# SwiGLU feed-forward on one core: the last 256 output columns move from VectorE and the SP queue to ScalarE and the ACT queue

## The chip, the cores and the metric

The kernel runs on one core of a Trainium2 chip. The metric is the device time of one execution in microseconds (us). One executed kernel gives one time. A profiled execution gives a trace as well, with the start and the duration of every instruction.

A few words are used throughout. The **span** is the time from the first to the last instruction in the trace, 121.1 us for the kernel before. The **tail** is the time from the end of the last matmul to the end of the span. A **semaphore** is a counter that one instruction raises and another waits for. A transfer has **landed** when its semaphore has its last count; the **closing** is the time from the landing of the last store to the end of the span. A **slab** is a block of weight columns that one transfer loads. The times outside the timeline views, given to the nanosecond below, are from the instruction records of the same traces (their starts, ends, semaphore waits and DMA landings).

## The reference

```python
# x: (1, 2048, 512), w_gate and w_up: (512, 1376), w_down: (1376, 512), all bfloat16
def reference(x, w_gate, w_up, w_down):
    g = jax.nn.silu(x @ w_gate)
    u = x @ w_up
    return (g * u) @ w_down
```

## The kernel before

The token axis is cut into four chunks of 512. For each chunk and each 128 columns of F, TensorE computes gate and up into two PSUM banks, ScalarE takes the Silu, VectorE multiplies, and the product stays in SBUF. Then come 16 output tiles of 128 tokens; each takes 11 matmuls, a copy out of PSUM, and a store. The last tile is cut into two groups of 256 columns, so that the last copy and store are short.

```python
N_WARM = 11
# ... (buffers and semaphores cut)
        o_groups = []                        # (tile, first column, columns)
        for t in range(NST):                 # NST = 16
            if t == NST - 1:
                o_groups.append((t, 0, HD))  # HD = 256
                o_groups.append((t, HD, HD))
            else:
                o_groups.append((t, 0, D))   # D = 512
        NOG = len(o_groups)                  # 17

        @block.sync
        def _(sp):
            xT_dma(sp, 0)                    # x, transposed on the way
            for si in range(len(slabs)):     # five slabs of gate and up columns
                wg_slab_dma(sp, si)
                wu_slab_dma(sp, si)
            # ... (the other loads cut)
            n_store = [0] * NOS              # NOS = 3 output buffers
            for gi, (t, c0, ncol) in enumerate(o_groups):
                ob = og_buf(gi)
                if gi == NOG - 2:
                    sp.wait_ge(s_Ofa, 1)     # ScalarE copied the next-to-last group
                elif gi == NOG - 1:
                    sp.wait_ge(s_Of, gi)
                else:
                    sp.wait_ge(s_Of, gi + 1)
                sp.dma_start(of[t * P:(t + 1) * P, c0:c0 + ncol],
                             o_sb[ob][:, c0:c0 + ncol]).then_inc(s_out[ob], 16)
                n_store[ob] += 1
            for i in range(NOS):             # the end waits for every buffer's stores
                sp.wait_ge(s_out[i], 16 * n_store[i])

        @block.tensor
        def _(pe):
            for i in range(N_WARM):          # warm-up matmuls on constants
                pe.matmul(banks[7][:, :], lhsT=ones_w, rhs=ones_m, start=True, stop=True)
            # ... for each chunk c and column tile ft:
            #     wait x chunk, wait gate slab, 4 matmuls; wait up slab, 4 matmuls
            # ... then 11 matmuls for each of the o_groups

        @block.scalar
        def _(act):
            # ... (the Silus cut)
            gi = NOG - 2                     # ScalarE copies the next-to-last group
            # ...
            act.activation(o_sb[ob][:, c0:c0 + ncol], psO[bb][:, 0:ncol], ACT.Copy).then_inc(s_Ofa, 1)

        @block.vector
        def _(dve):
            # ... (the products cut)
            for gi, (t, c0, ncol) in enumerate(o_groups):
                if gi == NOG - 2:
                    continue
                # ... waits
                dve.tensor_copy(o_sb[ob][:, c0:c0 + ncol], psO[bb][:, 0:ncol]).then_inc(s_Of, 1)
```

## Time and profile before

| what | value |
|---|---|
| time | 122.78 us, median of 3 runs (122.36 to 122.86) |
| span of the profiled run | 121.1 us |
| TensorE busy | 117.9 us, 97% |
| before the first real matmul | 5.5 us |
| from there to the end of the last matmul | 113.1 us |
| tail | 2.49 us |

First the page of the kernel before: the span, the busy time of each engine with its share and number of instructions, and the chain of waits that ended last.

```profile
span 121.1 us, 1391 instructions
## 1 busy us (share of the span) xinstructions
PE 117.9 (97%) x550; PEld 53.3 (44%) x550; DVE 43.8 (36%) x64; ACT 30.2 (25%) x51; POOL 0.2 (0%) x4
...
PE 97%; DVE 0%; issue 0%
```

TensorE is the limit, and nothing else comes near it. Next, the same kernel cut into three stretches, head, middle and tail (start:end, length, then busy time and instructions of each engine, the granted clock, the share and rate of the DMA):

```profile
0.00:5.50 5.50, 4.73 (x11) 1.47 (x11) 0.00 (x0) 1.49 (x2) 0.20 (x4) 1.00 0.71 154
5.50:118.66 113.16, 113.16 (x540) 51.79 (x539) 43.40 (x63) 28.74 (x49) 0.00 (x0) 1.00 0.24 67
118.66:121.15 2.49, 0.00 (x0) 0.00 (x0) 0.42 (x1) 0.00 (x0) 0.00 (x0) 1.00 0.18 53
```

In the middle TensorE is busy for the whole of the 113.16 us: no copy, Silu or store is waited for there. In the head it is busy too, but with eleven warm-up matmuls on constants. In the tail only one short copy is counted as busy; the rest is a store on its way. The tail in the timeline (start, length, engine; SPq is SyncE's DMA queue, and the length of a DMA line is the time to issue it, not to move the data), and the time to landing of that last store:

```profile
118.69 0.42 DVE L308 CAST o_sb<-bank 128x256 bf16<-128x256 f32 x1 [1.72 <-PE bank L245]
119.15 0.33 SPq L156 DMA_DIRECT2D out_dram<-o_sb  x1
```

```profile
out_dram<-o_sb SPq DMA_DIRECT2D x1, 64.0 KB, 1.5
```

The matmul ends at 118.655, the copy takes 0.425, the store is issued at 119.146 and lands at 120.667, and 0.480 us more pass until the last instruction of the closing barrier has ended. So a chain that the page counts as "0%" takes 2.49 us, and the chain of waits on the page stops at the copy.

### The profile page before, as it was taken

How to read it: one execution, taken by the hardware profiler on the slowest of the kernel's cores; microseconds unless marked ns; L12 is line 12 of the kernel's file. 1: busy time of each engine (PE TensorE's matmuls, PEld its weight loads, DVE VectorE, ACT ScalarE, POOL GpSimd, SP SyncE). 2: the span in 40 equal slices, each digit the busy share in tenths (PEclk: the TensorE clock that was granted, in tenths of full speed). 3: DMA queues.
4: the chain of work that ended last, by engine and by line, in shares of the span. 5: the costliest groups of instructions: out<-in, count | busy, mean ns of one | idle time of the engine just before them, and what ended most of it. 6: DMA issues, size and time to landing. Idle time of an engine off the chain costs nothing.

```text
span 121.1 us, 1391 instructions
## 1 busy us (share of the span) xinstructions
PE 117.9 (97%) x550; PEld 53.3 (44%) x550; DVE 43.8 (36%) x64; ACT 30.2 (25%) x51; POOL 0.2 (0%) x4
## 2 busy tenths in 40 slices
PE   7999999999999999999999999999999999999991
PEld 2244444444444444444444444444444444444470
DVE  0024334444334444334444334467242233224221
ACT  4032333262333272333262333230000000000010
POOL 0000000000000000000000000000000000000000
PEclk9999999999999999999999999999999999999999
DMA  3999999900000000000000000000211211121121
GB/s 67 255 283 372 262 241 225 369 20 0 0 0 0 0 0 5 0 0 3 3 0 0 0 0 0 5 0 0 87 43 43 87 43 49 49 81 43 43 74 56
DMA packets 17990, 8.51 MB, mean 70 GB/s; under 512 B 11360, under 2 KB 17984, under 8 KB 17984
## 3 DMA queue, kind: packets, MB, share of 16 engines
q1 hardware_dynamic: 17984, 8.42, 25.6%
q8 instruction: 4, 0.07, 0.2%
q14 instruction: 2, 0.02, 0.0%
HBM read 4.23 MB, written 2.10 MB: 52 GB/s over the span
## 4 chain that ended last, share of the span: by engine, by line
PE 97%; DVE 0%; issue 0%
PE bank L245 32%; PE bank L179 29%; PE bank L191 29%; PE bank L167 4%; PE bank L204 3%; PE bank L215 2%; DVE o_sb L308 0%; PE bank L220 0%
## 5 line engine op out<-in xcount | busy, mean ns | idle before, releaser
L284 DVE TENSOR_TENSOR hT_sb<-sg_sb,bank 128x512 bf16<-128x512 f32 x40 | 27.5, 688 | 44.9 <-PE bank L191 44.8
L179 PE MATMUL bank<-xT_sb,w_sb 128*128 128x512 bf16 x160 | 41.5, 382 | 0.0
L191 PE MATMUL bank<-xT_sb,w_sb 128*128 128x512 bf16 x160 | 41.1, 379 | 0.0
L245 PE MATMUL bank<-wd_sb,hT_sb 128*128 128x512 bf16 (+3 forms) x187 | 38.3, 367 | 0.0
L261 ACT ACTIVATE sg_sb<-bank 128x512 f32<-128x512 f32 x40 | 23.8, 596 | 44.7 <-PE bank L179 44.7
L245 PEld LDWEIGHTS bank<-wd_sb,hT_sb 128*128 128x128 bf16 (+1 forms) x187 | 18.1, 97 | 20.3 <-issue 0.4
L179 PEld LDWEIGHTS bank<-xT_sb,w_sb 128*128 128x128 bf16 x160 | 15.6, 98 | 19.8 <-DMA xT_sb<-in_x_dram 0.8
L191 PEld LDWEIGHTS bank<-xT_sb,w_sb 128*128 128x128 bf16 x160 | 15.6, 98 | 18.9
L308 DVE CAST o_sb<-bank 128x512 bf16<-128x512 f32 (+1 forms) x16 | 10.8, 675 | 24.9 <-PE bank L245 24.9
L275 ACT ACTIVATE o_sb<-bank 128x256 bf16<-128x256 f32 x1 | 0.4, 383 | 37.6 <-PE bank L245 37.6
L167 PE MATMUL bank<-const-bfloat16-1.0 128*128 128x512 bf16 x11 | 4.9, 628 | 0.8 <-PEq L322 0.8
L289 DVE TENSOR_TENSOR hT_sb<-sgx_sb,bank 32x512 bf16<-32x512 f32 x4 | 2.8, 692 | 5.3 <-ACT sgy_sb L266 5.3
L204 PE MATMUL bank<-xT_sb,w_sb 128*128 128x512 bf16 x16 | 4.1, 379 | 0.0
L265 ACT ACTIVATE sgx_sb<-bank 32x512 f32<-32x512 f32 x4 | 2.4, 588 | 4.5 <-PE bank L204 4.5
L167 PEld LDWEIGHTS bank<-const-bfloat16-1.0 128*128 128x128 bf16 x11 | 1.5, 140 | 3.3 <-issue 3.3
L296 DVE TENSOR_TENSOR hT_sb<-sgy_sb,bank 64x512 bf16<-64x512 f32 x4 | 2.7, 684 | 0.1
L204 PEld LDWEIGHTS bank<-xT_sb,w_sb 128*128 128x128 bf16 x16 | 1.6, 98 | 1.9
L266 ACT ACTIVATE sgy_sb<-bank 64x512 f32<-64x512 f32 x4 | 2.4, 589 | 0.0
L215 PE MATMUL bank<-xT_sb,w_sb 128*64 128x512 bf16 x8 | 1.9, 382 | 0.0
L220 PE MATMUL bank<-xT_sb,w_sb 128*64 128x512 bf16 x8 | 1.9, 382 | 0.0
L254 ACT ACT_TABLE_LOAD x1 | 1.3, 1283 | 0.7 <-PEq L322 0.7
L215 PEld LDWEIGHTS bank<-xT_sb,w_sb 128*64 128x64 bf16 x8 | 0.8, 110 | 1.0 <-issue 0.4
(6 smaller groups left out, 1.4 us busy)
## 6 DMA issues: line engine op xcount, KB each, us to landing
out_dram<-o_sb SPq DMA_DIRECT2D x15, 128.0 KB, 1.7
wd_sb<-in_w_down_dram SPq DMA_DIRECT2D x1, 1280.0 KB, 6.3
w_sb<-in_w_gate_dram SPq DMA_DIRECT2D x1, 480.0 KB, 6.2
w_sb<-in_w_up_dram SPq DMA_DIRECT2D x1, 448.0 KB, 6.8
w_sb<-in_w_gate_dram SPq DMA_DIRECT2D x1, 384.0 KB, 4.8
w_sb<-in_w_up_dram SPq DMA_DIRECT2D x1, 384.0 KB, 5.4
w_sb<-in_w_gate_dram SPq DMA_DIRECT2D x2, 128.0 KB, 3.1
w_sb<-in_w_up_dram SPq DMA_DIRECT2D x2, 128.0 KB, 3.0
```

The lines of the kernel that those rows point to most:

```text
L167: pe.matmul(banks[7][:, :], lhsT=ones_w, rhs=ones_m, start=True, stop=True)
L179: ins = pe.matmul(psG[n % NG][:, :], lhsT=w_sb[:, dk, ft * P:(ft + 1) * P], rhs=xT_sb[:, dk, c * SC:(c + 1) * SC], start=(dk == 0), stop=( ...
L191: ins = pe.matmul(psU[n % NU][:, :], lhsT=w_sb[:, dk, UPH + ft * P:UPH + (ft + 1) * P], rhs=xT_sb[:, dk, c * SC:(c + 1) * SC], start=(dk = ...
L204: ins = pe.matmul(psX[:, :], lhsT=w_sb[:, dk, XC0:XC0 + P], rhs=xT_sb[:, dk, c * SC:(c + 1) * SC], start=(dk == 0), stop=(dk == KD - 1),)
L215: pe.matmul(psY[pi][0:64, :], lhsT=w_sb[:, dk, YC0:YC0 + 64], rhs=xT_sb[:, dk, a * SC:(a + 1) * SC], start=(dk == 0), stop=(dk == KD - 1), ...
L245: ins = pe.matmul(psO[bb][:, 0:ncol], lhsT=hT_sb[0:K, fk, t * P:(t + 1) * P], rhs=wd_sb[0:K, fk, c0:c0 + ncol], start=(fk == 0), stop=(fk ...
L261: act.activation(sg_sb[n % NSG][:, :], psG[n % NG][:, :], ACT.Silu).then_inc(s_Gf, 1)
L265: act.activation(sgx_sb[c][96:128, :], psX[64:96, :], ACT.Silu)
L284: dve.tensor_tensor(hT_sb[:, ft, c * SC:(c + 1) * SC], sg_sb[n % NSG][:, :], psU[n % NU][:, :], ALU.mult,).then_inc(s_Uf, 1)
L289: dve.tensor_tensor(hT_sb[64:96, NFF, c * SC:(c + 1) * SC], sgx_sb[c][96:128, :], psX[96:128, :], ALU.mult,).then_inc(s_Xd, 1)
L296: dve.tensor_tensor(hT_sb[0:64, NFF, c * SC:(c + 1) * SC], sgy_sb[c][y0:y1, :], psY[pi][y0:y1, :], ALU.mult,).then_inc(s_Yd, 1)
L308: dve.tensor_copy(o_sb[ob][:, c0:c0 + ncol], psO[bb][:, 0:ncol]).then_inc(s_Of, 1)
```

## The change

What it can take is a little of the tail: ScalarE's copy of 256 columns takes 0.383 us in the trace and VectorE's 0.425, and the ACT queue saves handing the store to another engine. Most of the diff rewrites the kernel in a small recording layer, with one counting semaphore per engine and one per DMA. The instructions and their order on each engine stay as they were, except at the end (550 matmuls before and after). TensorE's separate semaphore instructions fall from 22 to 13. The core of the diff:

```diff
+class _Plan:                       # records operations with what they depend on
+    # ... op(), dma() cut
+    def emit(self, name, handle):
+        seen = {}
+        for o in self.lists[name]:
+            # ... collect the semaphores and counts that o.deps stand for
+            for k, (s, v) in need.items():
+                if seen.get(k, 0) < v:
+                    handle.wait_ge(s, v)
+                    seen[k] = v
+            # ... emit the instruction, then_inc its engine's or its DMA's semaphore
 ... (all operations rewritten as op(...) and dma(...) calls, in the same order)
-            gi = NOG - 2
-            act.activation(o_sb[ob][:, c0:c0 + ncol], psO[bb][:, 0:ncol], ACT.Copy).then_inc(s_Ofa, 1)
-                if gi == NOG - 2:
-                    continue
-                dve.tensor_copy(o_sb[ob][:, c0:c0 + ncol], psO[bb][:, 0:ncol]).then_inc(s_Of, 1)
-            for i in range(NOS):
-                sp.wait_ge(s_out[i], 16 * n_store[i])
+            last = gi == NOG - 1
+            cps = [copy("act" if last else "dve", c0, c0 + ncol)]
+            store("act" if last else "sp", 0, P, cps)
+            freed.append(cps)
+        for e in ("sp", "act"):
+            plan.lists[e].append(_Op(e, None, [s for t in range(NST - NOS, NST) for s in stores[t] if s.eng == e], False))
```

## The prediction

> **What bounds the kernel now.** TensorE. The page gives PE 117.9 us busy, 97% of a 121.1 us span, with the granted clock at full in every slice, and the chain of waits is 97% PE. In the trace's instruction records the matmuls start gap-free from 5.54 us to the last one, which ends at 118.655 us: 216 ns from start to start for 512 columns, 109 ns for 256, and only about 0.2 us lost in all, at the two places where the 64-column matmuls begin and end. Everything before 5.5 us (warm-up matmuls, first loads) and after 118.66 us is head and tail. The time of 122.78 us is the span plus about 1.7 us that the records do not cover.
>
> **What the change does.** The instruction order on each engine is the same before and after (550 matmuls, the same loads in the same order on the SP queue), except at the end. Most of the diff is a new recording layer: one counting semaphore per engine and one per DMA instead of named ones. TensorE has 22 separate semaphore instructions before and 13 after. As the present ones cause no gap in the matmul starts, removing nine of them is worth nothing. The three slots of the output tiles are waited for at the end before as well, so "the end waits only for the last three tiles" removes no wait that matters. What is left:
> - the next-to-last 256 columns are now copied by VectorE (before: ScalarE, 0.383 us). The last group's matmuls run 1.2 us after it, so this is hidden;
> - the last 256 columns are copied by ScalarE and stored from the ACT queue (before: VectorE, 0.425 us, stored from SP).
>
> **The tail, the only critical part that changes.** Before, from the timeline: last matmul ends 118.655; VectorE copy 118.693 to 119.118; SP issues the store at 119.146 and is busy 0.332 us; the store lands at 120.667 (1.52 us from issue); SP's branch, the drain and the barrier end at 121.147. After: ScalarE starts 0.037 us after its matmul in the present trace, takes 0.383, and its own queue should start the store about 0.03 us later: the store is issued some 0.04 us earlier. The Trainium skill (DMA: Bandwidth & Descriptors, "HWDGE ordering") says that SP and ACT own one ring each on the same 16 engines, so I expect the same 1.5 us to landing; its fixed cost (about 2 us, mostly the write receipt, same page) is not shortened by changing the queue, and the trace's 1.5 us is what I use. Against it: this is the first transfer on the ACT queue. On SP, the first plain load took 0.664 us to issue against 0.507 for later ones, and the first store 0.373 against 0.332, so a cold issue may cost 0.04 to 0.2 us. Net: -0.04 + 0.1 us, that is, nothing that three runs spreading over 0.5 us can show.
>
> **Predicted: 122.8 us, 8 in 10 between 122.3 and 123.3.** Faster by over 2%: 0.01; within 2%: 0.98; slower by over 2%: 0.01.
>
> **What would show each step.** Matmuls from about 5.5 to 118.7 us without gaps, as before; ACT copy of 128x256 at about 118.7 us, 0.38 us long; one 64 KB issue from the ACT queue at 119.1 us, 0.33 to 0.5 us long, landing about 1.5 us later; span 121.0 to 121.4 us; SP's own last store landed by 119.5 us, so the closing barrier waits on ACT.
>
> **What would make it wrong.** A slow first issue or landing on the ACT queue (over 0.5 us extra); a fixed cost outside the span for using a second queue; the new semaphores opening gaps between matmuls, for instance a wait now tied to a later count of the same engine; a later start of the first real matmul, which would shift everything.

## More of the kernel before

One more stretch will matter: the first real weight loads of TensorE in the timeline of its weight loads (in brackets, how long the engine sat idle, and what ended it), and the first gate slab's time from issue to landing.

```profile
4.57 0.15 PEld L167 LDWEIGHTS bank<-const-bfloat16-1.0 128*128 128x128 bf16 x1 [0.28 <-issue]
5.51 0.14 PEld L179 LDWEIGHTS bank<-xT_sb,w_sb 128*128 128x128 bf16 x2 [0.79 <-DMA xT_sb<-in_x_dram]
5.92 0.15 PEld L179 LDWEIGHTS bank<-xT_sb,w_sb 128*128 128x128 bf16 x1 [0.28 <-issue]
6.35 0.11 PEld L179 LDWEIGHTS bank<-xT_sb,w_sb 128*128 128x128 bf16 x1 [0.28 <-issue]
6.58 0.10 PEld L191 LDWEIGHTS bank<-xT_sb,w_sb 128*128 128x128 bf16 x1
```

```profile
w_sb<-in_w_gate_dram SPq DMA_DIRECT2D x1, 128.0 KB, 3.2
```

The loads follow one another at about 0.43 us until 6.35 and then at 0.22: the array runs at half speed at first. And the bracket blames the load of x for the wait, but that matmul waits for two loads: x landed at 4.92 us, the gate slab at 5.405 (2.20 plus 3.2). The semaphore instruction for the slab passed at 5.433, so the slab, not x, let TensorE go. A wait for several semaphores has to be checked against the landings.

## The result

| | before | after |
|---|---|---|
| time, median (lowest to highest), 4 runs each | 122.82 us (122.36 to 122.95) | 122.67 us (122.49 to 122.91) |
| ratio | | 0.9999, 95% interval 0.9975 to 1.0022 |
| span of the profiled run | 121.147 us | 121.034 us |
| end of the last matmul | 118.655 us | 118.548 us |
| tail | 2.492 us | 2.486 us |

A ratio is the mean time of one kernel's runs over the mean of the other's in the same rounds, so it is not quite the ratio of the medians. The page of the kernel after:

```profile
span 121.0 us, 1373 instructions
## 1 busy us (share of the span) xinstructions
PE 117.1 (97%) x540; PEld 53.3 (44%) x550; DVE 43.8 (36%) x64; ACT 30.2 (25%) x51; POOL 0.2 (0%) x4
...
PE 97%; issue 1%; ACT 0%
```

The 0.8 us less of PE time is no gain: ten matmul records are missing (x540 against x550), and in nine of the ten places the starts are 432 ns apart, two steps of 216 (the tenth lies beside the 64-column matmuls). The weight loads are all there. The tail and the landing of its store, then TensorE's first weight loads and the first gate slab:

```profile
118.58 0.38 ACT L254 ACTIVATE o_sb<-bank 128x256 bf16<-128x256 f32 x1 [38.85 <-PE bank L247]
119.00 0.37 ACTq L259 DMA_DIRECT2D out_dram<-o_sb  x1
```

```profile
out_dram<-o_sb ACTq DMA_DIRECT2D x1, 64.0 KB, 1.6
```

```profile
5.56 0.14 PEld L166 LDWEIGHTS bank<-xT_sb,w_sb 128*128 128x128 bf16 x2 [0.84 <-DMA xT_sb<-in_x_dram]
5.97 0.60 PEld L166 LDWEIGHTS bank<-xT_sb,w_sb 128*128 128x128 bf16 x3 [0.28 <-issue]
```

```profile
w_sb<-in_w_gate_dram SPq DMA_DIRECT2D x1, 128.0 KB, 3.3
```

Term by term, the copy is 41 ns shorter, the store takes 62 ns longer from issue to landing (of which 38 in the issue itself), and the closing is 28 ns shorter. These sum to -7 ns, and the tails differ by -6. The hand-over from the copy to the store, which the ACT queue was to save, took 28 ns before and 30 after. The last matmul, however, ended 107 ns earlier although the first real one had started 47 ns later. From the ninth real weight load to the end of the last matmul both kernels take 111.21 us. So that difference arose before the ninth load, where TensorE has the same instructions in the same order in both.

**Theory.** The tail is a chain of copy, issue, landing and closing, all of it on the critical path; the change shortens one term and lengthens another. The layer is free. What else differs is the head, which varies from run to run. **Rivals.** (1) The layer gives something back to TensorE and the new tail takes it. (2) The tail is not what ends the program. (3) The landing is only noise, not a matter of the queue.

### The profile page after: what moved, and what is told of

Same layout as the page of the kernel before. It is cut to its first block, busy times and chain, and to the rows that moved or that the text cites. A ratio compares the mean times of both kernels' runs of the same rounds, so it can differ in the third digit from the quotient of the medians.

```text
span 121.0 us, 1373 instructions
## 1 busy us (share of the span) xinstructions
PE 117.1 (97%) x540; PEld 53.3 (44%) x550; DVE 43.8 (36%) x64; ACT 30.2 (25%) x51; POOL 0.2 (0%) x4
## 4 chain that ended last, share of the span: by engine, by line
PE 97%; issue 1%; ACT 0%
PE bank L166 60%; PE bank L247 31%; PE bank L163 4%; PE bank L221 2%; ACT o_sb L254 0%
## 5 line engine op out<-in xcount | busy, mean ns | idle before, releaser
L166 PE MATMUL bank<-xT_sb,w_sb 128*128 128x512 bf16 x330 | 72.6, 380 | 0.3
L221 PE MATMUL bank<-xT_sb,w_sb 128*64 128x512 bf16 x16 | 1.9, 382 | 0.0
```

The lines of the kernel that those rows point to most:

```text
L166: return op("pe", lambda e: e.matmul(bank[:, :], lhsT=w_sb[:, dk, col0:col0 + P], rhs=xT_sb[:, dk, c * SC:(c + 1) * SC], start=(dk == 0), ...
L221: ym = op("pe", lambda e, pi=pi, dk=dk, c=c, y0=y0, y1=y1: e.matmul(psY[pi][y0:y1, :], lhsT=w_sb[:, dk, YC0:YC0 + 64], rhs=xT_sb[:, dk, c ...
```

## The experiments

Twelve kernels were run, in three batches of four; the four of a batch share a chip and the runs of the kernel before. All gave correct results. The terms of the tail are collected here, in ns, from the instruction records; the issue is part of the time from issue to landing, and what a row lacks to its tail are two hand-overs (matmul to copy, copy to issue), together 62 to 70 ns in every row.

| kernel | copy | issue | issue to landing | landing to end | tail |
|---|---|---|---|---|---|
| before | VectorE 425 | SP 332 | 1521 | 480 | 2492 |
| after | ScalarE 384 | ACT 370 | 1583 | 452 | 2486 |
| tail_only | ScalarE 384 | ACT 374 | 1575 | 448 | 2474 |
| queue_only | VectorE 426 | ACT 371 | 1586 | 448 | 2530 |
| copy_only | ScalarE 383 | SP 332 | 1533 | 555 | 2533 |
| copy_only_order | ScalarE 383 | SP 333 | 1527 | 476 | 2449 |
| old_tail_new_layer | VectorE 425 | SP 332 | 1529 | 554 | 2573 |
| wait_all | ScalarE 384 | ACT 369 | 1574 | 443 | 2469 |
| warm_queue | ScalarE 384 | ACT 339 | 1549 | 443 | 2443 |
| last_512 | ScalarE 597 | ACT 374 | 1744 | 448 | 2855 |
| last_128 | ScalarE 278 | ACT 369 | 1505 | 444 | 2294 |
| combined | ScalarE 278 | ACT 338 | 1472 | 444 | 2260 |

### tail_only: the tail without the layer

```diff
 # the kernel before
-            gi = NOG - 2
+            gi = NOG - 1
             act.activation(..., ACT.Copy).then_inc(s_Ofa, 1)
+            act.wait_ge(s_Ofa, 1)
+            act.dma_start(of[...], o_sb[ob][...]).then_inc(s_outa, 16)
+            act.wait_ge(s_outa, 16)
 # VectorE now skips group NOG - 1, SP stores groups 0 to NOG - 2
```

> The kernel before with the new tail written by hand (VectorE copies the next-to-last 256 columns, ScalarE the last, stored from the ACT queue), old semaphores. Define the tail as the time from the end of the last matmul to the end of the span: 2.49 us before (118.655 to 121.147), 2.49 us after (118.548 to 121.034). My theory (the tail is a chain of copy, issue, landing and closing barrier, in which a shorter copy and a slower landing cancel): tail 2.49 us within 0.05, copy 0.384, issue on ACT about 0.37, landing 1.58 after the issue; time ratio 1.000 within 0.003. Rival (the new semaphore layer gives TensorE 0.1 us back and the new tail costs as much): the last matmul ends at 118.6 or later, and the tail is 0.1 us longer.

Measured: tail 2.474 us, copy 0.384, issue 0.374, landing 1.575; ratio 1.0002 (0.9982 to 1.0021), median 122.71 against 122.64. All is as the theory has it. The rival expected that the last matmul would end at 118.6 or later without the layer; it ended at 118.314, earlier than in before or after. The reason is the head: the first real load started at 5.561 and the array was at full speed at once. From the ninth load to the end of the last matmul it took 111.213 us, as before. There is nothing left for the layer to explain.

### queue_only: VectorE copies, the ACT queue stores

```diff
 # the kernel after
-            cps = [copy("act" if last else "dve", c0, c0 + ncol)]
+            cps = [copy("act" if gi == NOG - 2 else "dve", c0, c0 + ncol)]
```

> The kernel after, but the last 256 columns are copied by VectorE again (ScalarE takes the next-to-last 256) while the store stays on the ACT queue: the queue part of the change alone. My theory: copy 0.425 us, landing 1.58 us after the issue, tail 2.53 us (0.04 more than after). Rival (the copying engine makes no difference to the chain, or the landing varies by 0.06 us from run to run whatever the queue): tail 2.49 us or a landing of 1.52 us. Time ratio to before 1.000 within 0.003 in either case.

Measured: copy 0.426, landing 1.586, tail 2.530 us; the tail and its terms are as expected, and 0.04 us of copy shows in the tail one for one. The ratio was 1.0021 (1.0002 to 1.0040), within the stated 0.003 but higher than a tail 0.04 us longer than before accounts for (0.0003). The profiled run had a mishap in the head besides: two weight slabs landed late, and TensorE stood for about 0.24 us in all at 9.3 us. Load order and queue are those of after. Whether the other runs had it is not known, so the rest of that 0.2% is left open.

### copy_only: ScalarE copies, the SP queue stores

```diff
 # the kernel after
-            store("act" if last else "sp", 0, P, cps)
+            store("sp", 0, P, cps)
```

> The kernel after, but the last store is issued on the SP queue again while ScalarE copies the last 256 columns: the copy part alone. My theory: copy 0.384, issue 0.33, landing 1.52, tail 2.45 us (0.04 less than before or after). Rival (landing time is noise, not the queue): tail anywhere from 2.45 to 2.52 us, with a landing not tied to the queue. Time ratio 1.000 within 0.003.

Measured: copy 0.383, issue 0.332, landing 1.533, all as the theory has them, so rival 3 falls: in the runs up to here the 64 KB stores on SP land in 1.52 to 1.55 us, the ones on ACT in 1.575 to 1.586. But the tail was 2.533, not 2.45: the closing took 0.555 instead of 0.480. The ratio was 1.0014 (0.9988 to 1.0039). The records show why in outline: after the landing SP runs a separate semaphore instruction (120.648) and then the branch (120.727), where before only the branch followed the landing. The next experiment tests this.

### copy_only_order: which instruction waits for the last store

```diff
 # copy_only
-            plan.lists[e].append(_Op(e, None, [s for t in ... for s in stores[t] if s.eng == e], False))
+            plan.lists[e].append(_Op(e, None, [s for t in ... for s in stores[t] if s.eng == e][::-1], False))
```

> copy_only again, with the final waits of SP listed in the other order, so that the last store's semaphore is waited for by the branch that ends the block and not by a separate semaphore instruction ahead of it. copy_only missed its expected tail (2.533 against 2.45 us) although copy, issue and landing were as expected; its trace has a wait instruction, then the branch, after the landing, and 0.555 us from landing to the end against 0.480 before. Theory A (the order of the waits costs the 0.075): landing to end 0.48, tail 2.45 to 2.47 us. Theory B (four waits instead of three cost it, whichever comes last): 0.55 again.

Measured: landing to end 0.476, tail 2.449 us. Theory A holds: with the same four waits in another order, 0.08 us are gone, and copy_only's expected tail of 2.45 is met. In these traces a block's final waits are carried by separate semaphore instructions and by the branch that ends the block; a wait that ends on a separate instruction pays for the branch after it. The Trainium skill (Perfetto Trace Analysis, "Identifying Dependency Chains") says that such semaphore instructions may be put in ahead of an instruction that waits on several engines. The trace shows the like ahead of a branch that has several stores to wait for, and prices it here.

### old_tail_new_layer: the layer without the tail

```diff
 # the kernel after
-            cps = [copy("act" if last else "dve", c0, c0 + ncol)]
-            store("act" if last else "sp", 0, P, cps)
+            cps = [copy("act" if gi == NOG - 2 else "dve", c0, c0 + ncol)]
+            store("sp", 0, P, cps)
```

> The kernel after with the old tail (ScalarE copies the next-to-last 256, VectorE the last, both stored from SP): the recording layer and its semaphores alone. Before, after, tail_only, queue_only and copy_only all took 102.146 to 102.148 us from the fiftieth real weight load to the end of the last matmul. My theory: the same 102.15 here, and a tail made of before's terms: copy 0.425, issue 0.332, landing 1.52; with 0.555 from landing to end (four waits in copy_only's order), tail 2.57. Rival (the layer moves the matmuls): 102.1 or less, or 102.2 or more.

Measured: 102.148 us from the fiftieth load (counted from nought, as in the expected text) to the end of the last matmul, and a tail of 2.573 us, as summed. Rival 1 falls: the layer does not move a matmul, and the nine removed semaphore instructions were worth nothing. The one look (123.17 us) fell on the latest gate slab of all traces, landed at 5.954 us.

### wait_all: the end wait undone

```diff
 # the kernel after
-[s for t in range(NST - NOS, NST) for s in stores[t] if s.eng == e]
+[s for t in range(NST) for s in stores[t] if s.eng == e]
```

> The kernel after, waiting at the end for the stores of all sixteen tiles instead of the last three: the end wait undone. My theory: the thirteen more waits run on SP before the last store (on the ACT queue, which gates the barrier) has landed at 1.58 us after its issue, so the tail stays 2.44 to 2.49 us. Rival (each wait instruction costs about 0.05 us at the end): six or seven more of them, tail 2.8 us.

Measured: tail 2.469 us. The thirteen more waits ran on SP, and SP had reached the barrier at 119.75, while the store on ACT landed at 120.62. Here waiting for fewer stores is worth nothing, since another engine ends last.

### warm_queue: is the ACT queue slower, or only its first transfer?

```diff
 # the kernel after
-            store("act" if last else "sp", 0, P, cps)
+            store("act" if last or t == NST - 4 else "sp", 0, P, cps)
```
(The final wait takes in tile 12 as well.)

> The kernel after, with the store of tile 12 also issued from the ACT queue, some 8 us before the last one, so that the last store is no longer the first transfer there. In after, tail_only and queue_only the ACT store took 0.370 to 0.374 us to issue and 1.575 to 1.586 to land; 64 KB stores on SP took 0.332 and 1.52 to 1.55. Theory A (my prediction's cold issue): the last issue falls to 0.33 and the landing to about 1.52, tail 2.43 us. Theory B (the ACT queue is slower every time): issue 0.37 and landing 1.58 again, tail 2.48 us, and the store of tile 12 about 0.06 slower to land than its 128 KB neighbours at 1.70.

The tail in the timeline of warm_queue (start, length, engine):

```profile
118.73 0.38 ACT L254 ACTIVATE o_sb<-bank 128x256 bf16<-128x256 f32 x1 [38.85 <-PE bank L247]
119.14 0.34 ACTq L259 DMA_DIRECT2D out_dram<-o_sb  x1
```

The last issue fell from 0.37 to 0.34 us, the landing from 1.58 to 1.549, the tail to 2.443; the store of tile 12, now the first on the queue, took 0.374 to issue. That is mostly theory A: the issue comes within 7 ns of SP's 332, and the coldness is worth about 0.03 us. combined repeats this with 32 KB: against last_128 the issue falls from 369 to 338 ns and the time to landing from 1505 to 1472. All of it lies in the issue. Counted from the end of the issue, the 64 KB store of this run lands after 1.210 us and that of after, cold, after 1.213. The other ACT stores of 64 KB have 1.201 to 1.215, those on SP 1.189 to 1.201 and once 1.220. So after the issue a difference of about 0.01 us between the queues may be there, but it is not clear of the scatter, and it is left open. SP was cold too: its first store, 64 us after its last load, took 0.372 to 0.378 us to issue in every trace, the second 0.349 or 0.350, later ones 0.332 or 0.333. For the store of tile 12 theory B expected 0.06 more to landing; it took 1.745 against 1.687 to 1.705 for its neighbours on SP, but this was the cold one, so it does not tell the two apart. An ACT queue used once, some 116 to 118 us earlier, lies between cold and warm: 0.361 to issue in gate_act_warm9 and 0.352 in gate_on_act (1.567 and 1.558 to landing), and 0.354 for the store of tile 14 in combined. Whether it is the time since the last use or the number of uses that counts was not tested.

### last_512 and last_128: the size of the last group

```diff
 # the kernel after, last_512
-        o_groups = [(t, 0, D) for t in range(NST - 1)] + [(NST - 1, 0, HD), (NST - 1, HD, HD)]
+        o_groups = [(t, 0, D) for t in range(NST)]
 # the kernel after, last_128
+        o_groups = [(t, 0, D) for t in range(NST - 1)] + [(NST - 1, 0, 384), (NST - 1, 384, 128)]
```

> The kernel after, but the last tile is one group of 512 columns, copied by ScalarE and stored from the ACT queue in one transfer of 128 KB: the tail's work doubled. My theory (all of the tail counts): copy about 0.60 us (as the Silu of 512 columns takes 0.596), landing about 1.7 to 1.75 us (as the other 128 KB stores), tail 2.85 to 2.90 us, so span and time up by about 0.38 us, a ratio near 1.003. Rival (the end of the program is set by something else, so that the tail's size is free): span and time unchanged, within 0.1 us.

> The kernel after, with the last tile cut into 384 and 128 columns, so that the last copy and store are half as large. By the line through 512 columns (0.597) and 256 (0.384) the copy should take 0.28 us; the store of 32 KB about 1.50 to landing; tail 2.29 to 2.32 us, 0.18 less than after. Theory A (matmul time goes with the columns: 0.109 us for 256, 0.216 for 512, so 0.163 and 0.056): the last matmul ends as before and the time falls by 0.18 us, ratio 0.9985. Theory B (a 128-column matmul cannot start faster than its weight load of 0.098 us): eleven of them cost 0.4 to 0.5 us more and the time rises by 0.2 to 0.3 us, ratio 1.002.

The tail in the timeline of last_512, then of last_128:

```profile
118.65 0.60 ACT L254 ACTIVATE o_sb<-bank 128x512 bf16<-128x512 f32 x1 [38.82 <-PE bank L247]
119.28 0.37 ACTq L259 DMA_DIRECT2D out_dram<-o_sb  x1
```

```profile
118.58 0.33 SPq L259 DMA_DIRECT2D out_dram<-o_sb  x1
118.61 0.28 ACT L254 ACTIVATE o_sb<-bank 128x128 bf16<-128x128 f32 x1 [38.85 <-PE bank L247]
118.92 0.37 ACTq L259 DMA_DIRECT2D out_dram<-o_sb  x1
```

last_512: tail 2.855 us, as summed; ratio 1.0037 (1.0017 to 1.0058), median 123.22 against 122.64. Rival 2 falls: what is added to the tail shows in the time. last_128: tail 2.294 us, as summed, and the matmuls of 128 columns start 55 to 56 ns apart, so its theory A holds and theory B falls: weight loads of 98 ns overlap and do not hold them up, and from the ninth load to the end TensorE took 111.212 us, nothing more. The ratio of last_128 was 0.9969 (0.9952 to 0.9987), median 122.46 against 122.81. The expected 0.9985 is inside the interval. Against before the tail explains 0.2 us of the gain; the rest of the mean is no more than the interval allows for.

### gate_act_warm9 and gate_on_act: the head

All traces of the kernels that load the first gate slab on SP show the first real weight load 0.104 or 0.105 us after that slab has landed, and the slab landed anywhere from 5.39 to 5.95 us. It is issued second, after the transpose of x, whose issue takes 1.4 us. So:

```diff
 # the kernel after, both
-            g = load_w("sp", w_gate, 0, a * P, min(b * P, F))
+            g = load_w("act" if a == 0 else "sp", w_gate, 0, a * P, min(b * P, F))
 # gate_act_warm9 only
-N_WARM = 11
+N_WARM = 9
```

> The kernel after, with the first gate slab loaded from the ACT queue at the start, beside the x transpose on SP, and 9 warm-up matmuls instead of 11. In all six traces the first real matmul's weight load starts 0.104 us after this slab lands (5.405 to 5.795 us), while x has landed at 4.80 to 4.99. Theory A (the head is set by that landing): the slab lands before x, TensorE starts at 4.9 to 5.1 us, and the span falls by 0.25 us (if the clock step to 216 ns comes late, since half-speed matmuls gain half) to 0.8 us; ratio 0.994 to 0.998, with still no gap later. Theory B (the transpose is slowed by the load beside it, or the later slabs come too late, or fewer warm-up matmuls delay the clock step): gaps or a late step take it back, ratio 0.999 or more.

> The head's change without the fewer warm-up matmuls: the first gate slab on the ACT queue, 11 warm-up matmuls. x lands at 4.8 to 5.05 us, the slab at about 3.1. While the clock is slow the last warm-up starts at 4.99 and takes 0.427. Theory A (the warm-up matmuls themselves now stand in the way): the first real matmul starts at 5.42 us when the clock steps late, and at 4.95 to 5.15 when it steps early; ratio 0.996 to 0.998, less gain than with 9. Theory B (the slab was all that mattered): the same 0.996 or less.

From the start of gate_act_warm9's timeline: the transpose, the slab beside it, and the first real weight load.

```profile
0.73 1.41 SPq L123 DMA_TRANSPOSE xT_sb<-in_x_dram  x1
0.73 0.43 ACTq L131 DMA_DIRECT2D w_sb<-in_w_gate_dram  x1
...
5.08 0.13 PEld L166 LDWEIGHTS bank<-xT_sb,w_sb 128*128 128x128 bf16 x2 [1.23 <-DMA xT_sb<-in_x_dram]
```

gate_act_warm9: the slab landed at 3.062, and this time the bracket is right: x landed at 5.042 and the first load started at 5.083. No later gap. Ratio 0.9959 (0.9944 to 0.9974), median 122.35 against 122.81: theory A. gate_on_act: ratio 0.9965 (0.9948 to 0.9982), median 122.29 against 122.69; the first real load at 5.324, 0.041 us after x, which landed at 5.283. So x came later than the 5.05 us that was expected at most. It set the start, not the warm-up matmuls, and the start is none of those that theory A named. With overlapping intervals from different batches the two do not settle whether 9 warm-up matmuls are better than 11. But theory B of the first has a true part. In the three traces that load the slab beside the transpose, x lands at 5.04, 5.28 and 5.28 us; in the eleven others at 4.80 to 5.00. It does not take the gain back: the first real load starts at 5.24 us in the mean of these three traces and at 5.68 in that of the eleven, and the difference of 0.44 us is about what the two ratios give (0.43 and 0.50).

### combined: all of it

```diff
 # the kernel after
-N_WARM = 11
+N_WARM = 9
-            g = load_w("sp", w_gate, 0, a * P, min(b * P, F))
+            g = load_w("act" if a == 0 else "sp", w_gate, 0, a * P, min(b * P, F))
-        ... + [(NST - 1, 0, HD), (NST - 1, HD, HD)]
+        ... + [(NST - 1, 0, 384), (NST - 1, 384, 128)]
-            store("act" if last else "sp", 0, P, cps)
+            store("act" if last or t == NST - 2 else "sp", 0, P, cps)
-            [s for t in range(NST - NOS, NST) for s in stores[t] if s.eng == e]
+            [s for t in range(NST - NOS, NST) for s in stores[t] if s.eng == e][::-1]
```

> All that the runs found, on top of after: the first gate slab on the ACT queue with 9 warm-up matmuls, the last tile cut 384 and 128, the store of tile 14 also on the ACT queue so that the last is not a cold one (warm_queue: issue 0.339 and landing 1.549 against 0.370 and 1.583), and the last store's semaphore waited for last. If the gains are independent terms of one sum (head 0.4 us, tail 0.2 us): first real matmul at 5.0 to 5.2, last matmul to end 2.24 to 2.27 us, 22 ns per 128-column set as in last_128, time 122.0 to 122.3, ratio 0.993 to 0.996. If they collide (the ACT queue's transfers or the 384-column store of SP in the way of the last store): tail 2.35 or more.

Measured: ratio 0.9951 (0.9932 to 0.9970), median 122.13 us (121.94 to 122.63) against 122.69; tail 2.260 us. Its end in the timeline:

```profile
118.35 0.28 ACT L254 ACTIVATE o_sb<-bank 128x128 bf16<-128x128 f32 x1 [38.85 <-PE bank L247]
118.66 0.34 ACTq L259 DMA_DIRECT2D out_dram<-o_sb  x1
```

It beats the kernel before by about half a per cent, which the interval puts clear of 1, though under the 2% that would be called faster. The expected start of 5.0 to 5.2 was missed: 5.324, because x landed at 5.282. The "22 ns per 128-column set" in the expected text was an error of mine; TensorE's middle took 111.214 us, with no extra. On the same chip combined and gate_on_act have means of 122.20 and 122.34 us, 0.14 apart where the tails differ by 0.2; with six runs of each, spread over 0.6 us, this agrees with a sum of the two gains but does not prove it.

## Why the prediction was right

**The whole.** 122.8 us was predicted (122.3 to 123.3, 0.98 for "within 2%"); 122.67 was measured.

**TensorE bounds the kernel, and the layer is worth nothing: right.** The stretch from the ninth load to the end of the last matmul takes 111.211 to 111.213 us in every kernel with the same groups, except queue_only with its late slabs. old_tail_new_layer and tail_only each hold one half of the change, and neither moves it.

**The shorter copy, -0.04 us: right.** It was -0.041, and queue_only against after shows that it is worth exactly that in the tail (0.044 us).

**The ACT queue's first transfer, +0.04 to +0.2 us: right as a term, at its low end.** The issue cost 0.038 more, and warm_queue, with the queue used before, takes back 0.031 of it. The prediction left the time to landing at 1.5 us; it was 1.58, 0.062 more in all with the issue counted. The other 0.024 us came after the issue, where warm_queue takes nothing back; what it is stays open.

**The closing barrier: its length not foreseen.** The prediction said rightly that it would wait on ACT, but kept SP's closing as it was. In both kernels only the branch still waits when the store lands, and from there to the end it took 0.452 us on ACT against 0.480 on SP. copy_only_order shows that another 0.08 us can lie in which instruction carries the last wait. This term of -0.028, and a first transfer of 0.062 instead of 0.1, make the expected -0.04 + 0.1 us into -0.006. That they all but cancel is luck. It is below what the times can resolve.

**A fixed cost outside the span for using a second queue: a danger named, and none found.** Where time and span are of one execution, which is so for all the kernels but before, the time is 1.78 to 1.80 us longer, whether the stores go from SP alone (1.785 to 1.803) or from the ACT queue too (1.782 to 1.797).

**"The end wait removes no wait that matters": right.** wait_all waits for all sixteen tiles and has a tail of 2.469 us.

**"Matmuls to 118.7 us as before": right in substance, and close by luck.** They ended at 118.548, because the head ran differently. The prediction named a later start of the first real matmul as a danger, but did not say that the head already scatters by several tenths of a us, which is more than the change could give or take. The records hold two sources. One is the landing of the first gate slab, 5.39 to 5.95 us. The other is the moment when the matmul steps fall from 427 to 216 ns: from about 3.5 us after the span's start in copy_only_order to about 6.4 in before. In last_512 it is seen among the warm-up loads, in its timeline of weight loads, three of them within 0.58 us:

```profile
3.28 0.15 PEld L163 LDWEIGHTS bank<-const-bfloat16-1.0 128*128 128x128 bf16 x1 [0.28 <-issue]
3.71 0.58 PEld L163 LDWEIGHTS bank<-const-bfloat16-1.0 128*128 128x128 bf16 x3 [0.28 <-issue]
5.89 0.34 PEld L166 LDWEIGHTS bank<-xT_sb,w_sb 128*128 128x128 bf16 x3 [1.61 <-DMA xT_sb<-in_x_dram]
```

In before, the fourth real weight load at 6.35 still came at the slow step. The Trainium skill (TensorE: Matmul & The Clock Gate, "What's actually happening") ascribes such a step to a free-running activity window, which would make it a matter of the moment at which the kernel starts. That it moves between runs of the same code up to that point is shown here; its cause is not. The views print a granted clock of 1.00 in every stretch and do not show it. But the packed traces of eleven runs record when the full clock was granted, and it is at the step: 6.364 us in before, 6.110 in after, 3.787 in last_512. It then lasted 116.053 us in ten of them and 119.466 in last_512; these are 34 and 35 times 3.413 us, which hints at fixed windows.

The two sources account for the 107 ns between before and after. The first real matmul started 47 ns later (5.587 against 5.540). The stretch from it to the step was 0.523 us long against 0.824, and of what is run at half speed half is lost: 0.262 against 0.412, which is 0.150 less. That leaves -0.103 us of the -0.107 measured.

**Left open:** the 0.024 us after the issue on the ACT queue, the rest of queue_only's 0.2%, what moves the clock step, and what lies in the 1.8 us between span and time.

## What to carry to other kernels

Once the main engine is gap-free, a change at the end is worth what it takes from the sum copy + hand-over + issue + landing + closing; write all five terms down, for a queue that has not been used lately adds to the issue (0.03 us here), and the order of the last waits to the closing (0.08). Make the last group small (here 128 columns: -0.19 us of tail, at no cost in matmul time) rather than choosing the engine of its copy (-0.04). And look at the other end: the two loads that the first matmul needs were issued one after the other on one queue, and putting one on the idle queue gave 0.4%, ten times what the change was after.

## What the Trainium skill lacked or had wrong

- DMA: Bandwidth & Descriptors, "Anatomy of one DMA": its fit of about 2.0 us plus bytes at 436 GB/s is for transfers issued by GpSimd, and there is no such fit for SP and ACT. Here stores from SBUF took 1.52 to 1.55 us for 64 KB and 1.69 to 1.72 for the last four of 128 KB from issue to landing on SP, well under the 2.15 us that the fit gives for 64 KB.
- No page that was read for this has a cost for the first transfer of a queue, or the first in a long while: on ACT 0.369 to 0.374 us to issue for the first, 0.352 to 0.361 for one 116 to 118 us after another, and 0.338 to 0.339 for one 2 to 7 us after another.
- Perfetto Trace Analysis, "Identifying Dependency Chains", names the inserted semaphore instructions but gives no cost: 0.075 to 0.08 us here when the last landing is waited for by one of them instead of the branch.
- TensorE: Matmul & The Clock Gate, "Back-to-back issue gap", gives sustained spacings, weight loads included, of about 81 ns for 128 columns and 131 for 512, and calls N/2.4 + 2.5 ns the isolated one. In these streams of weight load and matmul the spacing was 55 to 56 ns for 128 columns, 109 for 256, 162 for 384 and 216 for 512, which is the second formula. An earlier section of the page has measured spacings that agree with it.
- The same page, "What you observe", puts the step to full speed at about 4 us of activity, within 0.5 us from run to run. With warm-up matmuls from 0.77 us, it came between about 2.7 and 5.6 us after the first of them. The page's next section does allow for such a scatter, in numbers of slow matmuls.
- VectorE: DVE Perf Modes, "The TRN2 errata": its table for copies from PSUM to SBUF, taken without a speed-up factor, gives estimates of 392 ns for 256 columns on VectorE and 357 on ScalarE. The trace has 425 and 384: the right order, 7 to 8% short.
